# Retention and MoE on one core: outer products of chunk 2 ahead of its neighbour's scores, two weight casts on other engines, one weight sum later

## The chip, the core and the metric

The kernel runs on one core of a Trainium2 chip. The core has TensorE (PE, matrix products; its weight loads are shown apart as PEld), VectorE (DVE), ScalarE (ACT), GpSimd (POOL) and SyncE (SP, which here only issues transfers), each with a queue of its own that runs in program order. On-chip data lie in SBUF; matrix products are written to PSUM tiles. The metric is the device time of one execution in microseconds, lower is better.

## The reference

Two layers follow each other: a retention layer, which keeps a decaying state per head and reads it out with q at every token, and a feed-forward layer with the activation h * tanh(softplus(h)).

```python
# q, k, v: 4 batches, 8 heads, 768 tokens, 64 wide
for t in range(S):
    state = gamma[None, :, None, None] * state + np.einsum('bhd,bhe->bhde', k[:, :, t], v[:, :, t])
    y[:, :, t] = scale * np.einsum('bhd,bhde->bhe', q[:, :, t], state)
# x = y as 3072 tokens x 512; w_in 512 x 2048, w_out 2048 x 512
h = x @ w_in
sp = np.where(h > 20.0, h, np.log1p(np.exp(np.minimum(h, 20.0))))
return (h * np.tanh(sp)) @ w_out
```

## The kernel before

**Tiling.** The 3072 tokens are 24 chunks of 128. Within a chunk retention is done in matrix form: scores k q masked to the past (`scores...`, `mask...`), the masked scores times v (`present...`), the state before the chunk times q (`past...`), and the outer products k v that advance the state (`outer...`, `state...`). The results y, transposed, are the input `xt` of the feed-forward layer. Chunks are grouped in blocks: the first has four chunks, the other ten have two. A block's first product with `w_in` goes to PSUM tiles `h_ps`, the activation is taken by ScalarE, and the product with `w_out` goes to `o_ps`. From block 1 on both products are done by a scheme of seven products instead of eight per 2x2 partition, for which sums of weights (`wsum` from `w_in`, `tmat` from `w_out`), of inputs (`xsum`) and of activations (`gsum`) are made beforehand by VectorE.

**Weights.** `w_in` comes as four slices of 512 columns (`load_w`), 1 MB each, in SyncE's queue behind q, k and v of the first chunks; slice 0 comes as two transfers of half a slice. Each slice is cast from 32 to 16 bits in two halves (`cast_win(s, half, engine)`), the tiles `win{s}_{half}`. The first block works through the slices in order: `first_g1(h_ps, u, s)` uses columns u * 128 of slice 0, so u = 0 and 1 need half 0, and u = 2 and 3 need half 1; the later slices are used by `g1(0, u)` for u = 4 to 15. `w_out` follows as four slices, cast by `cast_wout(s, part, on_act)`; a slice's staging tile is that of an earlier input slice, so that the transfer of output slice 0 waits until both halves of input slice 0 are cast.

**The order.** Everything is scheduled by hand: each engine runs its instructions as the Python code issues them, and semaphores order the engines among each other. The first block is written out in `first_block` and `first_g2`; later blocks take their small steps from tables. In `first_block` the prologue takes chunks 0 to 3 in pairs: the score products of a pair are done in two halves of the heads (`scores_half(s, half, at)`, L314), each into a PSUM tile `at` that is masked by VectorE (`mask_half`, L321). Two such tiles exist, so that the scores of one wait for the mask of the one before the last. `outer_first(s, chunks)` makes the outer products of the chunks of pair s (L333), from k cast by ScalarE and v scaled by GpSimd (`cast_two`, L288); `state_first(g)` adds the state before (L343) and decays it by VectorE (L345). `fourth_state` (L354, L361) makes the fourth chunk's state, which GpSimd decays (L366).

A list `late` holds VectorE's weight sums as work that is called off piecewise (`some_late(n)`): `win_sums(a)` gives eight steps for a = 0 and eight for a = 1, sixteen in all (L770), `weight_sums(half)` four (L722 to L725). A table `plan` says what is issued behind which u of the first block's products. In `first_g2`, behind two pairs of products, one finds a chain over two engines: VectorE's second weight sum (L723), GpSimd's `gate` on it (L427), which holds GpSimd's queue, and behind the gate the scaling of the next chunks' q (`cast_q`, L406), which TensorE then transposes (`turn`, L453).

Of the kernel before, what the change touches and what calls it, by code (L numbers as in the profile page):

```python
# [16 lines left out]
def kernel(  # L17
# [9 lines left out]
    nc = tc.nc  # L27
# [15 lines left out]
    NSL = 4  # L43
# [14 lines left out]
    def toks(c):  # L58
        return slice(c * HB, (c + 1) * HB)
# [83 lines left out]
    nload, late, early = [0], [], set()  # L143
    BRING = CPB
    stores = []
    last_ended, yet = [], []

# [49 lines left out]
    def cast_win(s, half, eng):  # L199
        src = wtmps["in", s]  # L200
        t = cpool.tile([P, NBP, TB // 2], FP16, name=f"win{s}_{half}")
        src = src[:, :, half * (TB // 2):(half + 1) * (TB // 2)]
        if eng is nc.scalar:
            nc.scalar.copy(t, src)
        else:
            eng.tensor_copy(t, src)
        wins[s, half] = t

    def cast_wout(s, f, on_act=False):
        if s not in wouts:  # L210
            wouts[s] = cpool.tile([P, FPS, d_model], FP16, name=f"wout{s}")
        dst, src = wouts[s][:, f], wtmps["out", s][:, f]
        if on_act:
            nc.scalar.copy(dst, src)
        else:
            nc.vector.tensor_copy(dst, src)
# [110 lines left out]
    def outer_first(s, chunks=(0, 1)):  # L327
        u_ps = {c: mmps.tile([P, HP, P], FP32, name="u_ps", tag="mm") for c in chunks}
        for i in range(HP):
            half, j = divmod(i, HP // 2)  # L330
            for r in range(R):
                for c in chunks:
                    nc.tensor.matmul(  # L333
                        u_ps[c][:, i], k16s[s][toks(c), half, r, 2 * j:2 * j + 2],
                        v16s[s, half][toks(c), r, 2 * j:2 * j + 2],
                        start=i == 0 and r == 0, stop=r == R - 1, skip_group_check=True)
        for c in chunks:
            us[2 * s + c] = u_ps[c]

    def state_first(g):  # L340
        u = us.pop(g)
        if g > 0:
            nc.tensor.matmul(u, ident, states[g - 1], start=False, stop=True, skip_group_check=True)  # L343
        states[g] = stp.tile([P, HP, P], FP16, name="st")
        nc.vector.tensor_tensor(states[g], u, gcm, op=ALU.mult)  # L345
# [88 lines left out]
    def at_tile():  # L434
        return atps.tile([P, 2, HP // 2, R, C], FP32, name="at", tag="at")
# [271 lines left out]
    def some_late(n):  # L707
        for _ in range(min(n, len(late))):
            late.pop(0)()
# [351 lines left out]
    def first_block():  # L1061
# [50 lines left out]
        for half in range(2):  # L1112
            cast_two("v", 1, half)
        cast_win(0, 0, nc.gpsimd)
        at = at_tile()
        scores_half(1, 1, at)
        mask_half(1, 1, at)
        y = [atps.tile([P, 2, HP, C], FP32, name="y_ps", tag="at")[:, 0] for _ in range(2)]
        outer_first(1, [0])
        state_first(2)  # L1120
        h_ps = [mmps.tile([P, 1, TB], FP32, name="h_ps", tag="mm") for _ in range(2)]
        for u in range(2):
# [1 line left out]
        present_first(1, y, range(HP))  # L1124
        past_first(2, y)
        past_first(3, y)
        cast_win(0, 1, nc.vector)
        xt_out_by_two(2, y)
        for u in range(2, FPS):
            h_ps.append(mmps.tile([P, 1, TB], FP32, name="h_ps", tag="mm"))  # L1130
# [13 lines left out]

        def more_sums():
            late.extend(win_sums(1))
            some_late(8)
            late.extend(weight_sums(0) + weight_sums(1))

        plan = {6: [(cast_win, NSL - 1, 0, nc.scalar)],  # L1150
                7: [(cast_win, NSL - 1, 1, nc.scalar), (more_sums,)],
                9: [(cast_wout, 0, slice(0, 3)), (cast_wout, 0, slice(3, 4), True), (room_for_more,),
                    (bring_first,)],
                10: [(some_late, 1)],
# [30 lines left out]
    def first_g2():  # L1185
# [33 lines left out]
        for p in pairs:  # L1219
            mm(pe[p], sm(p, 1), t(1), True)  # L1220
            nc.scalar.copy(m5[p], pe[p])
        cast_wout(2, slice(0, 2))
        cast_wout(2, slice(2, 4), True)
        some_late(1)
        gate(tmats[0][:, 1, 0, :1])
# [193 lines left out]
```

## Time and profile before

| | |
|---|---|
| times of three runs | 191.51, 190.88 and 306.08 us, median 191.51 |
| the profiled execution | 190.88 us, of them 189.0 us from the first to the last instruction |
| TensorE busy | 182.5 us, 97% of the span |
| VectorE, ScalarE, GpSimd busy | 155.6, 126.8 and 95.3 us |
| granted TensorE clock | 1.000 |
| chain that ended last | 91% TensorE |

The profile is of one execution. Lines of the timeline give the start in us from the span's beginning, the length in us, engine, line of the code, operation, tiles, shapes and count; in square brackets stands the idle time of the engine just before and what ended it. Neighbouring instructions of a kind are merged to one row. A PE matmul's row may overlap the next, since products are pipelined. Rows of the chain give start, length and work. Rows of the stretches give, for each, its length and the busy time and count of instructions by engine, the granted clock, the DMA share and the rate.

### The profile page before, as it was taken

To read this page: it belongs to the slowest core of one execution; us is meant where nothing else is said; L and a number is where in the kernel's file an instruction comes from. 1 tells how busy PE (TensorE), PEld (TensorE's weight loads), DVE (VectorE), ACT (ScalarE), POOL (GpSimd) and SP (SyncE) were. 2 spreads that over 40 slices of the span, in tenths; PEclk is the share of its full clock that TensorE was granted. 3 is DMA by queue.
4 is the path that set the end of the run, shared out by engine and by line. 5 is a ranking of instruction groups with operands and counts; after the bars stand their busy time and mean duration, and the time that the engine had idled before them with its cause. 6 is when DMAs were issued, how large, how long until landed. Compare 5 with 4: busy or idle time off the path is not lost.

```text
span 189.0 us, 7724 instructions
## 1 busy us (share of the span) xinstructions
PE 182.5 (97%) x3283; PEld 155.8 (82%) x3283; DVE 155.6 (82%) x329; ACT 126.8 (67%) x249; POOL 95.3 (50%) x135
## 2 busy tenths in 40 slices
PE   7789999999999999999999999999999999999992
PEld 3457546975988988988988988988988989989981
DVE  3997899879899699797897897797897897796662
ACT  3462599385883983983983984974874974965960
POOL 6570107696878937924935925916916913000000
PEclk9999999999999999999999999999999999999999
DMA  5999999999999999999998995999996984300203
GB/s 165 351 368 405 404 407 279 278 248 134 151 192 251 180 285 210 208 219 177 167 194 146 188 187 158 197 195 120 178 203 117 148 144 59 114 0 17 101 0 111
DMA packets 95521, 36.17 MB, mean 191 GB/s; under 512 B 82560, under 2 KB 88960, under 8 KB 95488
## 3 DMA queue, kind: packets, MB, share of 16 engines
q1 hardware_dynamic: 74112, 32.78, 75.3%
q0 software_dynamic: 21088, 2.62, 22.4%
q8 instruction: 25, 0.41, 0.9%
q10 hardware_dynamic: 288, 0.30, 0.4%
q14 instruction: 8, 0.07, 0.1%
HBM read 27.30 MB, written 6.29 MB: 178 GB/s over the span
## 4 chain that ended last, share of the span: by engine, by line
PE 91%; DVE 3%; DMA 2%; POOL 1%; issue 1%; ACT 0%; SPq 0%; DVEq 0%; POOLq 0%
PE h_ps L820 34%; PE o_ps L956 32%; PE h_ps L687 6%; PE o_ps L1210 5%; DMA qfirst<-in_q_dram 2%; PE h_ps L1057 2%; PE o_ps L1275 2%; PE y_ps L532 2%; PE u_ps L483 2%; PE at L497 2%; DVE am L321 2%; PE y_ps L543 2%; POOL qfirst L249 1%; DVE osb L977 1%; PE at L314 0%
## 5 line engine op out<-in xcount | busy, mean ns | idle before, releaser
L840 DVE TENSOR_TENSOR hsum<-h_ps,hsnap 128x512 f32<-128x512 f32 x60 | 38.5, 685 | 10.1 <-ACT hsnap L830 6.6
L830 ACT COPY hsnap<-h_ps 128x512 f32<-128x512 f32 x60 | 32.1, 589 | 10.3 <-PE h_ps L820 10.1
L820 PEld LDWEIGHTS <-wsum 128*128 128x128 f16 x640 | 36.2, 98 | 0.1
L835 ACT ACTIVATE g<-hsum 128x512 f16<-128x512 f32 x60 | 34.6, 643 | 0.6 <-DVE hsum L840 0.2
L956 PEld LDWEIGHTS <-gsum 128*128 128x128 f16 x320 | 30.4, 98 | 3.7
L820 PE MATMUL h_ps<-xsum,wsum 128*128 128x128 f16 x480 | 30.2, 220 | 0.0
L956 PE MATMUL o_ps<-tmat,gsum 128*128 128x256 f16 x240 | 29.5, 273 | 0.0
L820 PEld LDWEIGHTS <-win 128*128 128x128 f16 x480 | 28.2, 98 | 0.9
L418 POOL DMA_DIRECT2D qk<-in_k_dram x36 | 27.5, 777 | 0.0
L956 PEld LDWEIGHTS <-g 128*128 128x128 f16 x248 | 22.7, 98 | 2.6
L406 POOL TENSOR_TENSOR qk<-qf,qvs 128x512 f16<-128x512 f32 x20 | 22.1, 1106 | 0.0
L956 PE MATMUL o_ps<-wout,g 128*128 128x256 f16 (+1 forms) x168 | 20.8, 268 | 0.0
L423 POOL TENSOR_TENSOR v<-vf,qvs 128x512 f16<-128x512 f32 x20 | 20.7, 1060 | 0.0
L820 PE MATMUL h_ps<-xt,win 128*128 128x128 f16 x320 | 19.6, 220 | 0.0
L550 ACT COPY hsum<-y_ps 128x512 f32<-128x512 f32 x9 | 5.3, 585 | 18.3 <-PE y_ps L543 18.3
L977 DVE TENSOR_TENSOR osb<-o_ps,snap 128x256 f32<-128x256 f32 (+1 forms) x32 | 13.0, 413 | 5.0 <-PE o_ps L956 2.4
L597 POOL TENSOR_TENSOR stc<-suc,gcv 128x256 f16<-128x256 f32 x15 | 9.9, 662 | 13.6 <-DVE suc L592 13.6
L427 POOL COPY gate<-gsum 128x1 f16<-128x1 f16 x10 | 1.9, 186 | 26.8 <-DVE gsum L927 26.8
L965 ACT COPY snap<-o_ps 128x256 f32<-128x256 f32 x31 | 11.4, 371 | 5.4 <-PE o_ps L956 5.0
L820 PE MATMUL h_ps<-xsum,win 128*128 128x128 f16 x160 | 12.3, 220 | 0.0
L820 PE MATMUL h_ps<-xt,wsum 128*128 128x128 f16 x160 | 12.2, 220 | 0.0
L835 ACT ACTIVATE g<-h_ps 128x512 f16<-128x512 f32 x20 | 12.0, 599 | 0.0
(144 smaller groups left out, 309.4 us busy)
## 6 DMA issues: line engine op xcount, KB each, us to landing
vf<-in_v_dram SPq DMA_DIRECT2D x24, 256.0 KB, 6.2
out_dram<-osb SPq DMA_DIRECT2D x22, 256.0 KB, 2.9
qf<-in_q_dram SPq DMA_DIRECT2D x20, 256.0 KB, 5.3
wi<-in_moe_w_in_dram SPq DMA_DIRECT2D x3, 1024.0 KB, 10.5
wt<-in_moe_w_out_dram SPq DMA_DIRECT2D x3, 1024.0 KB, 9.6
qk<-in_k_dram POOLq DMA_DIRECT2D x36, 64.0 KB, 5.1
qfirst<-in_q_dram SPq DMA_DIRECT2D x2, 512.0 KB, 4.3
kf<-in_k_dram SPq DMA_DIRECT2D x4, 256.0 KB, 4.9
```

The lines of the kernel that those rows point to most:

```text
L406: nc.gpsimd.tensor_tensor(by_head(g, room16(g)[0]), by_head(0, loaded[g][0]), f.broadcast_to((P, 2, HP, D)), op=ALU.mult)
L418: nc.gpsimd.dma_start(room16(g)[1][:, x::2], src[:, HP * x:HP * x + HP])
L423: nc.gpsimd.tensor_tensor(room16(g)[2], loaded[g][2], vs.unsqueeze(2).broadcast_to((P, H, D)), op=ALU.mult)
L597: by.tensor_tensor(stcs[g], sus.pop(g), decay, op=ALU.mult)
L687: nc.tensor.matmul(h_ps[:, j], win(s, f, bp), xt(blk, bp), start=(bp == 0), stop=(bp == NBP - 1))
L820: nc.tensor.matmul(h_ps[g][:, f], w(g, f, d), x(d), start=first and f == 0 and d == 0, stop=d == n - 1, skip_group_check=True)
L830: nc.scalar.copy(x, h_ps)
L835: nc.scalar.activation(gt[:, fb:fb + FPS, j * P:(j + 1) * P], h, AF.Mish, scale=inv_boost3)
L840: nc.vector.tensor_tensor(h, h_ps, x, op=ALU.add)
L956: nc.tensor.matmul(t, x(f), w(f)[:, c], start=first and f == 0, stop=f == n - 1, skip_group_check=True)
L965: nc.scalar.copy(x[:, c], t)
L977: nc.vector.tensor_tensor(dst[:, c], t, plus[:, c], op=ALU.add)
```

## The change

Five places move; no instruction is added or dropped, and no transfer changes its order.

1. `outer_first(1, [0])`, the outer products of chunk 2, stands ahead of `scores_half(1, 1, ...)` instead of behind its mask.
2. `cast_win(0, 1)`, slice 0's second half, is cast by GpSimd right behind the first half, instead of by VectorE behind the products of the states.
3. `cast_win(3, 1)`, slice 3's second half, is cast by VectorE instead of ScalarE, between the eighth and the ninth weight sum.
4. The last of the sixteen sums of `w_in` is put aside in a list `later`.
5. It is issued in `first_g2`, behind VectorE's half of output slice 2's cast.

```diff
-    last_ended, yet = [], []
+    last_ended, yet, later = [], [], []
...
         cast_win(0, 0, nc.gpsimd)
+        cast_win(0, 1, nc.gpsimd)
+        outer_first(1, [0])
         at = at_tile()
         scores_half(1, 1, at)
         mask_half(1, 1, at)
         y = [atps.tile([P, 2, HP, C], FP32, name="y_ps", tag="at")[:, 0] for _ in range(2)]
-        outer_first(1, [0])
         state_first(2)
...
         past_first(3, y)
-        cast_win(0, 1, nc.vector)
         xt_out_by_two(2, y)
...
         def more_sums():
             late.extend(win_sums(1))
-            some_late(8)
+            some_late(7)
+            later.extend(late)
+            late.clear()
             late.extend(weight_sums(0) + weight_sums(1))
...
-                7: [(cast_win, NSL - 1, 1, nc.scalar), (more_sums,)],
+                7: [(cast_win, NSL - 1, 1, nc.vector), (more_sums,)],
...
         cast_wout(2, slice(0, 2))
+        later.pop(0)()
         cast_wout(2, slice(2, 4), True)
```

On TensorE, in the prologue, before (`y_ps` is the result of chunks 0 and 1, `at` the score tile, `u_ps` the outer products, `v_389` and `v_391` the two halves of v, `st` the state; each pair of rows stands for several):

```order
L381 LDWEIGHTS st
L381 MATMUL y_ps<-qfirst_t,st 128x128
L314 LDWEIGHTS qkt
L314 MATMUL at<-qfirst_t,qkt 64x128
...
L333 LDWEIGHTS qk_293
L333 MATMUL u_ps<-v_389,qk_293 128x128
...
L333 MATMUL u_ps<-v_391,qk_293 128x128
L343 LDWEIGHTS ident
L343 MATMUL u_ps<-st,ident 128x512
```

and the same place with the change:

```order
L381 LDWEIGHTS st
L381 MATMUL y_ps<-qfirst_t,st 128x128
L333 LDWEIGHTS qk_293
L333 MATMUL u_ps<-v_389,qk_293 128x128
...
L333 MATMUL u_ps<-v_391,qk_293 128x128
...
L314 LDWEIGHTS qkt
L314 MATMUL at<-qfirst_t,qkt 64x128
...
L343 LDWEIGHTS ident
L343 MATMUL u_ps<-st,ident 128x512
```

The eight outer products now stand ahead of the sixteen score products, directly behind the results of chunk 1.

On VectorE, in the sums of `w_in` and what follows them, before (`win_0_565` and `win_1_573` are slice 3's halves, `win_1_515` is slice 1's second and `win_1_478` slice 0's second, `wout_600` output slice 0, `wout_702` output slice 2, `tmat` the sums of `w_out`):

```order
L770 TENSOR_TENSOR wsum<-win_1_478,wsum 128x2x256
L770 TENSOR_TENSOR wsum<-win_0_565 128x2x256
...
L770 TENSOR_TENSOR wsum<-win_1_515,win_1_573 128x2x256
L770 TENSOR_TENSOR wsum<-win_1_515,wsum 128x2x256
L216 COPY wout_600<-wt 128x1536
L722 TENSOR_TENSOR tmat<-wout_600 128x1024
...
L216 COPY wout_702<-wt 128x1024
L723 TENSOR_TENSOR tmat<-wout_702,tmat 128x1024
```

and with the change (slice 0's second half is `win_1_395` now, the output slices `wout_599` and `wout_701`):

```order
L770 TENSOR_TENSOR wsum<-win_1_395,wsum 128x2x256
L206 COPY win_1_573<-wi 128x1024
L770 TENSOR_TENSOR wsum<-win_0_565 128x2x256
...
L770 TENSOR_TENSOR wsum<-win_1_515,win_1_573 128x2x256
L216 COPY wout_599<-wt 128x1536
L722 TENSOR_TENSOR tmat<-wout_599 128x1024
...
L216 COPY wout_701<-wt 128x1024
L770 TENSOR_TENSOR wsum<-win_1_515,wsum 128x2x256
L723 TENSOR_TENSOR tmat<-wout_701,tmat 128x1024
```

Ahead of the ninth sum stands a cast more, and the sixteenth sum stands between the cast of output slice 2 and L723 instead of ahead of the cast of output slice 0.

On GpSimd, before the change and with it, one cast more stands ahead of the decay of the fourth state, `stc` (`win_0_393` and `win_1_395` are slice 0's halves):

```order
 L288 TENSOR_TENSOR v_391<-vf,qvs 128x4x2x64
 L206 COPY win_0_393<-wi 128x1024
+L206 COPY win_1_395<-wi 128x1024
 L366 TENSOR_TENSOR stc<-suc,gcf 128x256
 L427 COPY gate<-wt 128x1
```

The second cast directly follows the first.

## The prediction

> **What bounds the kernel now.** I read the page's busy shares and its chain that ended last first, then the stretches, then the timeline of each engine around the places that the change touches.
>
> ```profile
> PE 182.5 (97%) x3283; PEld 155.8 (82%) x3283; DVE 155.6 (82%) x329; ACT 126.8 (67%) x249; POOL 95.3 (50%) x135
> PEclk9999999999999999999999999999999999999999
> PE 91%; DVE 3%; DMA 2%; POOL 1%; issue 1%; ACT 0%; SPq 0%; DVEq 0%; POOLq 0%
> core 0: us, PE busy (x) PEld busy (x) DVE busy (x) ACT busy (x) POOL busy (x), PEclk, DMA share, GB/s
> 13.40:20.00 6.60, 6.30 (x114) 5.03 (x114) 5.18 (x8) 3.24 (x7) 1.07 (x2) 1.00 1.06 404
> 20.00:30.60 10.60, 10.56 (x54) 4.71 (x50) 9.98 (x23) 8.45 (x15) 2.34 (x3) 1.00 1.06 396
> 30.60:47.00 16.40, 16.40 (x195) 12.67 (x194) 14.28 (x22) 10.43 (x22) 12.49 (x13) 1.00 1.24 216
> 47.00:180.00 133.00, 133.00 (x2731) 122.69 (x2729) 112.06 (x234) 96.53 (x194) 70.63 (x99) 1.00 1.01 161
> ```
>
> TensorE is busy for 97% of the span at full clock, and the chain is 91% TensorE. From 20 us on it hardly pauses: 0.04 us are missing in 20 to 30.6, nothing in 30.6 to 180. Everything that the change touches lies before 52 us. So the change can win only where TensorE pauses now, and of the stretches it touches that is 13.4 to 20, with 6.60 - 6.30 = 0.30 us. It can lose wherever it makes TensorE wait in 14 to 47 us, where nothing waits today. A shift of TensorE at 47 us goes straight to the end, since no pause behind it absorbs it.
>
> The one pause, on TensorE's timeline, then the same place on the chain (start, length):
>
> ```profile
> 13.00 0.39 PE L381 MATMUL y_ps<-qfirst_t,st 128*128 128x128 f16 x4
> 13.70 0.42 PE L314 MATMUL at<-qfirst_t,qkt 64*64 64x128 f16 x16 [0.32 <-DVE am L321]
> 14.05 0.62 PE L333 MATMUL u_ps<-v,qk 64*128 64x128 f16 x8
> 14.12 0.55 PE u_ps L333 x8
> 14.67 0.32 PE u_ps L343
> 14.99 0.87 PE h_ps L1057 x8
> 12.44 1.22 DVE L321 TENSOR_TENSOR am<-at,tri_first 128x1024 f16<-128x1024 f32 x1
> 12.38 1.06 POOL L288 TENSOR_TENSOR v<-vf,qvs 128x512 f16<-128x512 f32 x1
> ```
>
> The score products of L314 write a PSUM tile that VectorE's mask (12.44 + 1.22 = 13.66) must have left; TensorE had been free since 13.38 and starts at 13.70, 0.04 us behind the mask's end. That 0.04 is my price for a hand-over between engines. The outer products (L333) stand behind the scores and need neither mask nor scores.
>
> **Outer products ahead of scores.** Nothing is added or removed: 8 products, 0.55 us on the chain. They need the second half of v, scaled by GpSimd until 12.38 + 1.06 = 13.44, so the last four may start at 13.48; the first four need no more than the first half and run from 13.38. They end at 13.93, the scores start then instead of at 13.70 (the mask is over at 13.66), and L343 starts at 14.35, not 14.67. **Gain 0.32 us**, or 0.17 if the second half of v came 0.15 later than the row says. The next to be late would be what VectorE does behind the scores:
>
> ```profile
> 14.17 1.22 DVE L321 TENSOR_TENSOR am<-at,tri_first 128x1024 f16<-128x1024 f32 x1
> 15.31 0.68 DVE L345 TENSOR_TENSOR st<-u_ps,gcm 128x512 f16<-128x512 f32 x1
> 15.91 0.68 DVE L206 CAST win<-wi 128x1024 f16<-128x1024 f32 x1
> 16.37 0.62 PE L381 MATMUL y_ps<-qfirst_t,st 128*128 128x128 f16 x8
> ```
>
> The last mask of the prologue now follows later scores: it starts near 14.40 and ends at 15.62, the state's product (L345) runs 15.54 to 16.22. TensorE wants the mask at about 15.8 (the second half of L374) and the state near 16.39 (the second four of L381, 0.32 earlier than today). Both are covered, by 0.15 us or so; if that cover is gone, TensorE waits the difference and the gain shrinks by it.
>
> **Slice 0, half 1: VectorE to GpSimd.** GpSimd's cast of the other half and the transfer that the new one needs:
>
> ```profile
> 13.48 1.04 POOL L206 CAST win<-wi 128x1024 f16<-128x1024 f32 x1
> 9.14 0.69 SPq L184 DMA_DIRECT2D wi<-in_moe_w_in_dram  x1
> wi<-in_moe_w_in_dram SPq DMA_DIRECT2D x1, 512.0 KB, 5.6
> 16.77 0.10 PEld L1057 LDWEIGHTS <-win 128*128 128x128 f16 x1
> 16.67 0.37 SPq L191 DMA_DIRECT2D wt<-in_moe_w_out_dram  x1
> wt<-in_moe_w_out_dram SPq DMA_DIRECT2D x1, 1024.0 KB, 9.6
> ```
>
> The half lands near 9.14 + 5.6 = 14.74; GpSimd is free at 14.52, casts until 15.8, and TensorE loads these weights at 16.77 - 0.32 = 16.45. Cost **0**, covered by 0.6 us. VectorE loses 0.68 us of work there, but it then waits for slice 1's transfer anyway, so that gains nothing. SyncE's first output slice, queued behind this cast, is issued at 15.9 instead of 16.67; it lands behind the input slices in either case (16.67 + 9.6 = 26.3), so I price it at 0, with 0.2 either way.
>
> **Slice 3, half 1: ScalarE to VectorE, and the sixteenth sum.** The cast leaves ScalarE (1.04 us each, no TensorE wait hangs on it) and lengthens VectorE's unbroken run from 21 to 35 us:
>
> ```profile
> 21.13 1.08 DVE L206 CAST win<-wi 128x1024 f16<-128x1024 f32 x1 [0.17 <-DMA wi<-in_moe_w_in_dram]
> 21.13 1.68 DVE L206 CAST win<-wi 128x1024 f16<-128x1024 f32 x2 [0.17 <-DMA wi<-in_moe_w_in_dram]
> 18.65 1.29 DVE L206 CAST win<-wi 128x1024 f16<-128x1024 f32 x2 [0.93 <-DMA wi<-in_moe_w_in_dram]
> 20.11 0.86 DVE L361 TENSOR_TENSOR suc<-u_ps,st 64x256 f32<-64x256 f32 x2 [0.16 <-PE u_ps L354]
> 21.05 0.61 POOL L366 TENSOR_TENSOR stc<-suc,gcf 128x256 f16<-128x256 f32 x1 [6.52 <-DVE suc L361]
> 28.45 0.42 DVE L770 TENSOR_TENSOR wsum<-win,wsum 128x512 f16<-128x512 f16 x1
> 28.79 0.95 DVE L216 CAST wout<-wt 128x1536 f16<-128x1536 f32 x1
> 30.44 0.69 DVE L1177 TENSOR_TENSOR gsum<-g 128x1024 f16<-128x1024 f16 x1
> 31.33 0.32 PEld L1210 LDWEIGHTS <-gsum 128*128 128x128 f16 x3
> ```
>
> A cast of this kind adds 1.68 - 1.08 = 0.60 us to the run, a sum 28.79 - 28.45 = 0.34. With one cast more and one sum fewer the first output cast (L216) is late by 0.26 us. Against that stands the row at 21.13: the same cast takes 0.68 elsewhere and 1.08 here, while GpSimd runs L366 beside it. L366 waits for VectorE's sum of the fourth state (L361, at 20.11), which waits for TensorE; with TensorE earlier it moves by 0.22 us (no more, since VectorE is at slice 1's casts, which a transfer starts, until about 19.9), and the overlap shrinks by as much. Bounds: nothing saved to 0.40 saved; I take 0.22, because the overlap is the nearest row to the excess. VectorE's run is then late by **0.04 us**, or 0.26 without it.
>
> The Trainium skill, page "SBUF — State Buffer", section "SBUF: two separate sides", says that GpSimd and a two-port VectorE operation hold a shared port pair for a whole instruction, the later one waiting. The rows agree in kind: 0.40 us too long, where GpSimd's span reaches 0.53 past the cast's start. By that rule the hold shrinks exactly as L366 moves and the sum is mine; without it nothing is saved, and the sum is that of the second rival.
>
> First consumer: the first sum of activations is done at 30.44 + 0.69 = 31.13 now, 31.17 then; its weights are loaded at 31.33, wanted 0.32 earlier, possible from 31.21. So **0.20 of the 0.32 is given back here**. Then the sixteenth sum:
>
> ```profile
> 33.12 0.68 DVE L216 CAST wout<-wt 128x1024 f16<-128x1024 f32 x1
> 34.05 0.69 DVE L723 TENSOR_TENSOR tmat<-wout,tmat 128x1024 f16<-128x1024 f16 x1 [0.25 <-ACT wout L214]
> 34.89 0.50 POOL L427 COPY gate<-tmat 128x1 f16<-128x1 f16 x1 [2.42 <-DVE tmat L723]
> 35.35 1.50 POOL L406 TENSOR_TENSOR qk<-qf,qvs 128x512 f16<-128x512 f32 x1
> 37.01 0.32 PEld L453 LDWEIGHTS <-qk 128*128 128x128 f16 x4
> ```
>
> It falls into VectorE's idle 0.25 us ahead of L723, but takes 0.34: free at 33.80 + 0.04, plus 0.34, L723 starts at 34.18, 0.13 late. GpSimd's gate waits for L723, the whole of GpSimd's queue waits behind the gate, and its first scaling of q ends at 35.35 + 1.50 + 0.13 = 36.98. TensorE loads that q at 37.01 today and could at 37.02. **The remaining 0.12 goes there.**
>
> Sum: -0.32 + 0.20 + 0.12 = 0.0, rounded (+0.01). The profiled execution took 190.88 us (span 189.0 and 1.9 around it), so it would again be 190.9. The median shown, 191.51, holds one run of 306; the two that agree have 191.2 as their mean, 0.3 above the profiled one. With that offset the forecast is **191.2 us**, no change.
>
> **Rivals**, with the same offset.
> 1. The gain survives: GpSimd's spans are rough, and the scaled q may have been ready 0.3 us before its row ends, the sum of activations likewise. For it: neither place shows a wait today. Against: the rows put both within 0.2 us of their use. 191.2 - 0.32 = 190.9 us.
> 2. The hold at 21.13 isn't L366's, and VectorE is late by 0.26 in full: weights at 31.44 instead of 31.33, L723 at 33.80 + 0.26 + 0.34 = 34.40, q ready at 37.24 against 37.01: 0.23 slower, 191.4 us. For it: one long row is thin evidence. The change failing at its own aim (the outer products waiting for v, so that L366 doesn't move) ends at the same number.
> 3. Slower: GpSimd's second cast holds up VectorE's last mask. It would run 14.74 to 15.8; a mask held until then ends at 17.0, where TensorE wants it at 15.8: 1.2 us of wait, less 0.32, 192.1 us. It decides once the mask ends after 15.8. Against: today's mask at 14.17 starts inside GpSimd's cast (13.48 to 14.52) and takes its usual 1.22.
>
> **How the numbers follow.** Forecast 0.45, gain survives 0.2, VectorE late in full 0.22, mask held 0.06; 0.07 for what I haven't seen, most of it a transfer or a queue falling out of step by microseconds. Executions differ by 0.6 us (190.88 to 191.51). The first three cases span 190.9 to 191.4; with 0.6 below and, for the third rival's side, 0.9 above, the range is 190.3 to 192.3. Two per cent, 3.8 us, is about what a measurement of this kernel can tell from no change; no case of mine reaches it. Faster by over 2%: 0.02; the pauses before 180 us don't hold 3.8 us that this change could reach. Slower: 0.05. Within: 0.93.
>
> **What would show it.** Right: the 0.32 us ahead of L314 is gone and L333 stands before L314 from 13.4; L343 near 14.35; GpSimd's two casts of L206 back to back, the second ending before 16; L366 near 20.8 and the cast beside it near 0.86 us; the loads of the sums (L1210) at 31.2; L723 near 34.2; the load of q (L453) at 37.0 again. Wrong: TensorE still 0.2 us or more ahead at 37 us (rival 1), a full 1.08 us cast and L453 at 37.2 (rival 2), a mask of over 2 us (rival 3). The forecast falls as a whole if TensorE shows a pause of over 1 us between 14 and 52 us, or the later stages pause at all.

## The result: 0.3% slower, through a wait that the prediction priced at 0.12 us

The changed kernel takes 191.78 us (median; before, beside it, 191.42). The ratio is **1.0031, 95% interval 1.0016 to 1.0045**, some 0.6 us of loss. The forecast was no change, 191.2 us in a range of 190.3 to 192.3: the time lies in the range, but the change has a sign, and the forecast had none. The interval is about half a us wide, so that far smaller changes than the 2% that the prediction named can be told here. Of 22 executions each, two of before (306 us) and one of after (367 us) were far longer and are not in the ratio. The profiled execution took 191.82 us, with a span of 190.1.

The page's busy shares and chain of the kernel after:

```profile
PE 182.5 (96%) x3283; PEld 155.2 (82%) x3283; DVE 155.0 (82%) x329; ACT 126.3 (66%) x248; POOL 95.3 (50%) x136
PE 78%; DVE 7%; DMA 6%; SPq 5%; POOL 1%; issue 1%; DVEq 0%; POOLq 0%
```

TensorE is busy for the same 182.5 us in a span 1.1 us longer: the loss is waiting. The chain fell from 91% TensorE to 78%: followed back, it now leaves TensorE near 38 us and goes through GpSimd and VectorE to a transfer. The stretches of the kernel after (length, busy time and count by engine) say where TensorE waits:

```profile
13.40:20.00 6.60, 6.58 (x114) 4.99 (x114) 4.71 (x8) 3.43 (x7) 2.09 (x3) 1.00 1.06 404
20.00:30.60 10.60, 10.60 (x53) 5.00 (x51) 9.82 (x23) 7.84 (x15) 2.36 (x4) 1.00 1.06 396
30.60:47.00 16.40, 15.71 (x188) 11.74 (x186) 13.20 (x21) 9.47 (x19) 11.50 (x12) 1.00 1.24 214
```

The pause of the first stretch is gone (6.58 busy instead of 6.30), but in 30.6 to 47 us, where TensorE never waited, 0.69 us are missing. TensorE's timeline of the kernel after, in the prologue and around 31 to 38 us:

```profile
13.30 0.62 PE L333 MATMUL u_ps<-v,qk 64*128 64x128 f16 x8
13.85 0.42 PE L314 MATMUL at<-qfirst_t,qkt 64*64 64x128 f16 x16
14.29 0.38 PE L343 MATMUL u_ps<-st,ident 128*128 128x512 f16 x1
...
30.16 1.04 PE L1212 MATMUL o_ps<-wout,g 128*128 128x256 f16 x8
31.32 1.05 PE L1212 MATMUL o_ps<-tmat,gsum 128*128 128x256 f16 x8
...
35.74 1.04 PE L1212 MATMUL o_ps<-tmat,gsum 128*128 128x256 f16 x8
36.61 0.60 PE L1212 MATMUL o_ps<-wout,gsum 128*128 128x256 f16 x4
37.78 0.40 PE L453 MATMUL t_ps<-ident,qk 128*128 128x128 f16 x4 [0.57 <-POOL qk L406]
```

Before, the same group stood at 36.68 (L1210 then, L1212 now) and the transposes of q at 37.11:

```profile
36.68 0.60 PE L1210 MATMUL o_ps<-wout,gsum 128*128 128x256 f16 x4
37.11 0.39 PE L453 MATMUL t_ps<-ident,qk 128*128 128x128 f16 x4
```

So 0.43 us became 37.78 - 36.61 = 1.17: **0.74 us lost at the transposes of q**, of which the row shows 0.57 as idle. The wait is for GpSimd's scaling of q. A smaller loss stands at 31.32: 1.16 us after the group ahead of it, which takes 0.87 where nothing waits (35.74 to 36.61 in the same profile), **0.29 us**.

GpSimd's timeline of the kernel after, from the prologue to that scaling, then VectorE's:

```profile
13.47 1.04 POOL L206 CAST win<-wi 128x1024 f16<-128x1024 f32 x1
14.84 1.04 POOL L206 CAST win<-wi 128x1024 f16<-128x1024 f32 x1 [0.33 <-DMA wi<-in_moe_w_in_dram]
20.84 0.61 POOL L366 TENSOR_TENSOR stc<-suc,gcf 128x256 f16<-128x256 f32 x1 [4.96 <-DVE suc L361]
35.03 1.71 POOL L427 COPY gate<-tmat 128x1 f16<-128x1 f16 x1 [3.77 <-DVE tmat L723]
36.69 1.03 POOL L406 TENSOR_TENSOR qk<-qf,qvs 128x512 f16<-128x512 f32 x1
```

```profile
21.11 1.50 DVE L206 CAST win<-wi 128x1024 f16<-128x1024 f32 x2 [0.35 <-DMA wi<-in_moe_w_in_dram]
...
33.26 0.69 DVE L216 CAST wout<-wt 128x1024 f16<-128x1024 f32 x1
33.86 0.42 DVE L770 TENSOR_TENSOR wsum<-win,wsum 128x512 f16<-128x512 f16 x1
34.19 0.68 DVE L723 TENSOR_TENSOR tmat<-wout,tmat 128x1024 f16<-128x1024 f16 x1
34.79 0.69 DVE L724 TENSOR_TENSOR tmat<-wout,wout 128x1024 f16<-128x1024 f16 x1
35.40 0.69 DVE L1185 TENSOR_TENSOR gsum<-g,gsum 128x1024 f16<-128x1024 f16 x1
36.00 0.69 DVE L725 TENSOR_TENSOR tmat<-wout,tmat 128x1024 f16<-128x1024 f16 x1
```

The gate copies one element per partition. Before, it took 0.50 us (34.89), and VectorE's L725 was the one that waited, 1.53 us long, beside the scaling of q. VectorE's row of before:

```profile
35.87 1.53 DVE L725 TENSOR_TENSOR tmat<-wout,tmat 128x1024 f16<-128x1024 f16 x1
```

Now VectorE's four operations L723 to L725 take their usual 0.68 to 0.69 each, and the gate lasts until the fourth is over (35.03 + 1.71 = 36.74; 36.00 + 0.69 = 36.69). The scaling of q starts only then. Its first half ends at 36.69 + 1.03 = 37.72 instead of 35.35 + 1.50 = 36.85, 0.87 us later: the gate starts 0.14 later with L723 and takes 1.21 more, and the scaling, with VectorE idle beside it, gives 0.47 back. The transposes had 0.2 us to spare and start 0.67 later (37.11 to 37.78); the group ahead of them stands 0.07 earlier (36.68 to 36.61), which makes the 0.74.

### The profile page after: what moved, and what is told of

Read it like the earlier page. It is cut to its first block, busy times and chain, and to the rows that moved or that the text cites. A ratio compares the mean times of both kernels' runs of the same rounds, so it can differ in the third digit from the quotient of the medians.

```text
span 190.1 us, 7725 instructions
## 1 busy us (share of the span) xinstructions
PE 182.5 (96%) x3283; PEld 155.2 (82%) x3283; DVE 155.0 (82%) x329; ACT 126.3 (66%) x248; POOL 95.3 (50%) x136
## 4 chain that ended last, share of the span: by engine, by line
PE 78%; DVE 7%; DMA 6%; SPq 5%; POOL 1%; issue 1%; DVEq 0%; POOLq 0%
PE h_ps L820 34%; PE o_ps L956 32%; DMA wi<-in_moe_w_in_dram 6%; SPq L270 3%; DVE wsum L770 3%; PE o_ps L1278 2%; PE y_ps L532 2%; PE o_ps L1212 2%; PE u_ps L483 2%; PE at L497 2%; PE y_ps L543 2%; DVE wout L216 1%; DVE win L206 1%; SPq L184 1%; POOL gate L427 1%
## 5 line engine op out<-in xcount | busy, mean ns | idle before, releaser
L406 POOL TENSOR_TENSOR qk<-qf,qvs 128x512 f16<-128x512 f32 x20 | 21.1, 1057 | 0.0
L956 PE MATMUL o_ps<-wout,g 128*128 128x256 f16 (+1 forms) x168 | 20.8, 267 | 0.0
L427 POOL COPY gate<-gsum 128x1 f16<-128x1 f16 x10 | 1.8, 184 | 26.7 <-DVE gsum L927 26.7
```

Of the source, the lines that this page charges most:

```text
L406: nc.gpsimd.tensor_tensor(by_head(g, room16(g)[0]), by_head(0, loaded[g][0]), f.broadcast_to((P, 2, HP, D)), op=ALU.mult)
L956: nc.tensor.matmul(t, x(f), w(f)[:, c], start=first and f == 0, stop=f == n - 1, skip_group_check=True)
```

## Experiments

In the table the ratio is to the kernel before (with its interval), *pause* is VectorE's idle time between its cast of output slice 2 and L723 (in the kernels with several sums there, between these), *gate* is the length of GpSimd's row of L427, *wait* is the idle time that TensorE's row of L453 shows. Pause, gate and wait are from one profile each.

| kernel | ratio | pause | gate | wait |
|---|---|---|---|---|
| before; before_again | | 0.25; 0.17 | 0.50 | 0 |
| outer_only | 1.0005 [0.9981, 1.0029] | 0.17 | 0.50 | 0 |
| cast3_on_scalar | 1.0004 [0.9979, 1.0029] | 0.10 | 0.50 | 0 |
| sum_in_place | 1.0022 [0.9996, 1.0047] | 0.10 | 0.50 | 0 |
| sum_first | 1.0032 [1.0007, 1.0058] | 0.10 | 0.50 | 0 |
| before_filled | 1.0039 [1.0018, 1.0059] | 0.23 | 0.50 | 0 |
| after_scalar_late | 1.0027 [1.0002, 1.0052] | 0.35 | 0.50 | 0 |
| before_three | 1.0080 [1.0054, 1.0106] | 0.03 twice | 0.50 | 0.29 |
| sum_twice | 1.0019 [0.9995, 1.0043] | 0.03 | 0.50 | 0.28 |
| two_later | 1.0017 [0.9993, 1.0041] | none | 0.50 | 0.16 |
| after; after_again; after_third | 1.0031 [1.0016, 1.0045]; one execution; 1.0068 [1.0038, 1.0097] | none | 1.71 | 0.57 |
| cast3_and_later | 1.0043 [1.0023, 1.0063] | none | 1.70 | 0.57 |
| pause_early | one execution | none | 1.71 | 0.57 |
| two_split | 1.0055 [1.0018, 1.0092] | none | 1.71 | 0.57 |
| three_later | 1.0036 [1.0014, 1.0058] | none | 1.71 | 1.03 |
| four_later | 1.0053 [1.0030, 1.0076] | none | 1.71 | 1.03 |

### Both kernels again

Neither is edited.

> The kernel before once more, for a second profile of it. Theory A (the gate on L723 is let in or kept out by VectorE's unbroken run of L723, L724, the fourth sum of activations and L725, and which of the two it is follows from the order of the work): the gate takes 0.50 us again and L453 comes at 37.1. Theory B (it is a matter of chance in each execution, in the kernel before as well): the gate may take 1.7 us here too, L453 then comes at 37.8 and the execution takes about 191.5 instead of 190.9. Theory C (the gate is not the cause): its length has no bearing on the time.

> The changed kernel once more. Theory A: the gate takes 1.7 us again and L453 comes at 37.8. Theory B: it may be let in, at 0.5 us, with L453 at 37.0 and a time near 190.9. Theory C: no relation between the two.

Measured 191.23 and 192.96 us, one execution each. The waits of TensorE from 13 to 180 us in after_again (engine, line, what it waited for, us, times, longest); before_again has none but that of L314 for the mask, 0.3 us:

```profile
PE t_ps L453 <- POOL qk L406: 0.6, 1, 0.6
PE o_ps L1212 <- DVE gsum L1179: 0.2, 1, 0.2
```

The two places of loss return, so they belong to the kernel and not to one execution. A third execution of the kernel after had them too:

> The changed kernel on the chip of the three others. Theory A: gate 1.7 us for the third time, wait at L453 0.5 to 0.7 us, ratio 1.003. Theory B: gate 0.5 us in this execution.

Measured 1.0068, gate 1.71, wait 0.57. The first profile also showed 0.3 us lost in the next block (VectorE's L724 held to 1.60 us by a scaling at 44.8); the two repeats don't show it (0.68 and 0.69 us), so it does not belong to the kernel.

### The outer products alone

The kernel before, with this edit only:

```diff
+        outer_first(1, [0])
         at = at_tile()
         scores_half(1, 1, at)
         mask_half(1, 1, at)
-        outer_first(1, [0])
```

> The kernel before with the outer products of chunk 2 ahead of the scores alone. All theories: TensorE is 0.2 to 0.3 us ahead at 20 us, with VectorE's run not later than before. Theory A: VectorE still has a pause ahead of L723, so the gate is let in, about 0.5 us, the q comes no later than before (L453 at 37.0), and the time is that of before, 0 to 0.2 us less. Theory B: the gate as often in as out, the times spread over 190.7 to 191.7 as those of before do. Theory C: the 0.2 to 0.3 us are gained, about 190.9 as a median.

TensorE's timeline of this kernel in the prologue and at the transposes of q:

```profile
13.77 0.62 PE L333 MATMUL u_ps<-v,qk 64*128 64x128 f16 x8
14.32 0.42 PE L314 MATMUL at<-qfirst_t,qkt 64*64 64x128 f16 x16
37.28 0.39 PE L453 MATMUL t_ps<-ident,qk 128*128 128x128 f16 x4
```

No wait is left anywhere between 13 and 180 us, yet the ratio is 1.0005 [0.9981, 1.0029]. From a group of transposes in the prologue (L299, at 10.98 here) to the first products of slice 0 (L687, at 20.36) TensorE took 9.38 us here and 9.32 in the kernel after, against 9.52 and 9.46 in the two profiles of before: of the 0.32 us, 0.1 to 0.2 reach 20 us, the rest goes into slightly wider spacing of the later products. In after_third and cast3_on_scalar TensorE also waited 0.4 us for an earlier mask (L374, at 13 us), ahead of the place that changed; why is open. Against an interval of half a per cent, 1 us, such a gain can't be seen.

### Slice 3's half back on ScalarE

The kernel after, with one word changed back:

```diff
-                7: [(cast_win, NSL - 1, 1, nc.vector), (more_sums,)],
+                7: [(cast_win, NSL - 1, 1, nc.scalar), (more_sums,)],
```

> The changed kernel with slice 3's second half on ScalarE again, the rest as changed. VectorE's run is 0.6 us shorter ahead of the output casts, so that L723 waits for ScalarE's cast of output slice 2 again. Theory A: with that pause the gate is let in (0.5 us), L453 near 37.0, time as before or 0.3 less, ratio to the kernel before 0.998 to 1.000. Theory B: in or out by chance, ratio 1.000 to 1.002. Theory C (the later weight sum or the second cast on GpSimd costs the time): ratio 1.003 as with the whole change.

GpSimd's and TensorE's timelines of this kernel:

```profile
35.51 0.50 POOL L427 COPY gate<-tmat 128x1 f16<-128x1 f16 x1 [2.60 <-DVE tmat L723]
```

```profile
37.30 0.60 PE L1212 MATMUL o_ps<-wout,gsum 128*128 128x256 f16 x4
37.73 0.39 PE L453 MATMUL t_ps<-ident,qk 128*128 128x128 f16 x4
```

The gate is back at 0.50 us, the transposes follow 0.43 us behind the group ahead of them as in the kernel before, the first sum is waited for no more, and the time is that of the kernel before. The sum still stands late here. So both waits hang on VectorE's cast of slice 3, as far as one profile shows; the interval of the ratio overlaps that of the kernel after.

### That cast and the late sum alone

The kernel before, with the change's parts 3 to 5 and neither the outer products nor slice 0:

```diff
-            some_late(8)
+            some_late(7)
+            later.extend(late)
+            late.clear()
...
-                7: [(cast_win, NSL - 1, 1, nc.scalar), (more_sums,)],
+                7: [(cast_win, NSL - 1, 1, nc.vector), (more_sums,)],
...
+        later.pop(0)()
```

> The kernel before with slice 3's half cast by VectorE and the sixteenth sum put off, and none of the rest of the change. By duration VectorE is 0.26 us late at the output casts and L723 0.3 us late, ratio 1.001 to 1.002. Theory A: the cast has used up VectorE's pause ahead of L723, the gate takes 1.7 us with a wait of 0.7 at L453, ratio 1.004 to 1.005. If the earlier prologue is needed for the loss: gate 0.5 us.

```profile
35.51 1.70 POOL L427 COPY gate<-tmat 128x1 f16<-128x1 f16 x1 [3.77 <-DVE tmat L723]
38.26 0.40 PE L453 MATMUL t_ps<-ident,qk 128*128 128x128 f16 x4 [0.57 <-POOL qk L406]
```

These are GpSimd's and TensorE's rows of this kernel. Without any change to the prologue, the whole wait is there, and the ratio is 1.0043 [1.0023, 1.0063]. The loss comes from these parts together.

### The sixteenth sum back in its place, or ahead of the cast

Both are edits of the kernel after. In the first (sum_in_place) all sixteen sums run together again; in the second (sum_first) the late sum and the cast change places:

```diff
-            some_late(7)
-            later.extend(late)
-            late.clear()
+            some_late(8)
...
-        later.pop(0)()
```

```diff
-        cast_wout(2, slice(0, 2))
         later.pop(0)()
+        cast_wout(2, slice(0, 2))
```

> The changed kernel with all sixteen weight sums together again, slice 3's half still cast by VectorE. VectorE reaches the output casts 0.34 us later than with the change, and L723 follows the cast of output slice 2 with no pause. Theory A (without a pause of VectorE ahead of L723 the gate is kept out until the run ends): gate 1.7 us, its wait at L453 0.6 to 0.8 us; and the wait for the first sum of activations grows from 0.3 to 0.6 us; ratio to the kernel before 1.004 to 1.006. Rival D (it is the sixteenth sum just ahead of L723 that keeps the gate out): the gate is let in, 0.5 us, ratio 1.002 to 1.003.

> The changed kernel with two of VectorE's instructions swapped: the sixteenth sum ahead of the cast of output slice 2 instead of behind it. Same work, same L723 but for 0.1 us: it now directly follows the cast whose result it reads, which in the profile of the variant with all sums together cost a pause of 0.1 us. Theory A (a pause of VectorE ahead of L723 decides): the gate is let in, 0.5 us instead of 1.7, no wait at L453, while the wait of 0.3 us for the first sum of activations stays; TensorE is 0.6 to 0.7 us earlier at 47 us than with the change, ratio to the kernel before 0.999 to 1.002. Theory B (chance, or the sum's mere presence): gate 1.7 us, ratio 1.003.

VectorE's and GpSimd's rows of sum_in_place, and the one wait of its TensorE:

```profile
34.28 0.68 DVE L216 CAST wout<-wt 128x1024 f16<-128x1024 f32 x1
35.06 0.69 DVE L723 TENSOR_TENSOR tmat<-wout,tmat 128x1024 f16<-128x1024 f16 x1
35.91 0.50 POOL L427 COPY gate<-tmat 128x1 f16<-128x1 f16 x1 [4.54 <-DVE tmat L723]
32.34 1.05 PE L1210 MATMUL o_ps<-tmat,gsum 128*128 128x256 f16 x8 [0.35 <-DVE gsum L1177]
```

In sum_in_place I had expected the gate at 1.7 and missed: with nothing between the cast and L723, which reads what the cast wrote, VectorE pauses 0.10 us (34.28 + 0.68 to 35.06), and the gate came in at 0.50. The loss stands at the first sum of activations instead, 0.35 us, since VectorE's run is a whole cast longer. In sum_first the same pause let the gate in, and TensorE waited 0.21 us for the later cast. So keeping the gate short doesn't win the time back: a VectorE that is late costs 0.2 to 0.35 us wherever its first result is awaited.

### A pause taken away, or put in

Three kernels try the pause ahead of L723 directly. Before_filled and before_three are the kernel before with the sixteenth sum repeated once, or three times, ahead of L723. The edit of before_three (before_filled puts one copy in the list, `twice.append(late[-1])`, and runs it once):

```diff
-    last_ended, yet = [], []
+    last_ended, yet, twice = [], [], []
...
             late.extend(win_sums(1))
+            twice.extend([late[-1]] * 3)
             some_late(8)
...
         cast_wout(2, slice(0, 2))
+        for again in twice:
+            again()
```

After_scalar_late is the kernel after with a redundant copy that makes ScalarE's half of the cast, and so L723, later:

```diff
+        nc.scalar.copy(wouts[2][:, 2:4, :384], wtmps["out", 2][:, 2:4, :384])
         cast_wout(2, slice(2, 4), True)
```

> The kernel before with nothing but the sixteenth weight sum done a second time between VectorE's cast of output slice 2 and L723, 0.34 us of work where VectorE pauses for 0.17 to 0.25 us. By duration alone L723 comes 0.1 to 0.2 us later and TensorE 0 to 0.2. Theory A: the pause is gone, the gate takes 1.7 us instead of 0.5, L453 comes 0.7 to 0.8 us later with a wait shown, ratio 1.003 to 1.004. Theory B (duration alone): gate 0.5 us, ratio 1.000 to 1.001. Rival E (the gate depends on the work ahead of the output casts, as with slice 3's half): gate 0.5 us.

> The changed kernel with work added: ScalarE casts 768 of the 1024 columns of its part of output slice 2 once more ahead of the whole, 0.7 us, so that VectorE pauses about 0.3 us ahead of L723. By duration alone this can only make L723 0.3 us later and the kernel as slow or slower, ratio 1.003 to 1.005. Theory A: the pause lets the gate in, 0.5 us instead of 1.7, q comes 0.3 to 0.4 us earlier than with the change, ratio 1.000 to 1.002. Rival D: the gate stays out, since the sixteenth sum is still there, ratio 1.004 to 1.005.

> The kernel before with three needless repetitions of the sixteenth weight sum ahead of L723, 1.0 us of work where one was not enough to fill VectorE's pause. By duration L723 comes 0.75 us later with the pause of 0.25 used up, the q by as much, less the 0.1 us of slack: 0.65 us at L453 with the gate at 0.5 us, ratio 1.003. Theory A: no pause, so the gate takes 1.7 us, and the q comes 1.4 to 1.5 us later than before, ratio 1.006 to 1.008.

Before_filled says nothing on the question: L723 waited 0.23 us for ScalarE all the same. Its ratio of 1.0039 comes without a long gate or a wait at L453, and its cause is open. In after_scalar_late the pause of 0.35 us was made and the gate took 0.50, but TensorE then waited 0.27 us for that same cast. VectorE's and GpSimd's rows of before_three:

```profile
34.07 1.34 DVE L770 TENSOR_TENSOR wsum<-win,wsum 128x512 f16<-128x512 f16 x3
35.32 0.68 DVE L723 TENSOR_TENSOR tmat<-wout,tmat 128x1024 f16<-128x1024 f16 x1
36.16 0.50 POOL L427 COPY gate<-tmat 128x1 f16<-128x1 f16 x1 [4.68 <-DVE tmat L723]
```

L723 starts inside the last sum's row, so there is no pause right ahead of it, and the gate still came in. That refuted the theory as I had it, that a pause directly ahead of L723 decides. But the three repeats write the same tile, and three sums that overlapped as others do (0.34 apart, 0.42 long) would take 1.10 us, not 1.34: there are two pauses of some 0.03 us between them. The ratio of 1.0080, 1.5 us, goes with a run of VectorE that is longer by the three sums, 1.3 us, and two waits of TensorE, 0.17 us for a sum of activations and 0.29 for q; where the rest of the 1.5 us goes was not found.

### Where the pause has to be

All three are edits of the kernel after. Sum_twice issues the late sum twice (a pause of 0.03 us between the two); two_later puts the fifteenth sum aside as well, so that two run late without a pause; pause_early has two repeats five operations ahead of L723, behind the cast of output slice 1:

```diff
+        later[0]()
         later.pop(0)()
```

```diff
-            some_late(7)
+            some_late(6)
...
         later.pop(0)()
+        later.pop(0)()
```

```diff
+        def last_sum():
+            later[0]()
...
-                13: [(cast_wout, 1, slice(0, 3)), (g_sum, 2), (g_sum, 3)],
+                13: [(cast_wout, 1, slice(0, 3)), (last_sum,), (last_sum,), (g_sum, 2), (g_sum, 3)],
```

> The changed kernel with the sixteenth sum done twice in a row behind VectorE's cast of output slice 2. The second writes what the first wrote and waits for it, so that VectorE pauses for some 0.04 us one operation ahead of L723; L723 itself comes 0.46 us later than with the change. Theory A2 (the gate is let in when VectorE has paused within the last two or three operations, kept out when its run is unbroken for longer): gate 0.5 us in spite of the added work, L453 at about the time of the changed kernel or up to 0.25 us earlier, ratio to the kernel before 1.003 to 1.005. Theory G (the number of operations between the cast and L723 decides, or their being sums): cannot be told from this run alone, see the next.

> The changed kernel with the fifteenth sum put off beside the sixteenth: the same work, two sums between the cast of output slice 2 and L723, which do not wait for each other. VectorE reaches the output casts 0.34 us earlier than with the change and L723 at the same time. Theory A2: the run is unbroken, gate 1.7 us, wait at L453 0.6 us, ratio 1.002 to 1.004 (the wait for the first sum of activations is gone, that for q is not). Theory G: gate 0.5 us as in the run with two sums that wait for each other, ratio 1.000 to 1.001.

> The changed kernel with the sixteenth sum done twice in addition, in a row, behind the cast of output slice 1: a pause of 0.04 us there, five operations ahead of L723, and no pause behind it. Theory A2: gate 1.7 us, since the pause lies too far back. If any pause in the run will do: 0.5 us. The time is not read here, since VectorE's work ahead of the sums of activations is 0.8 us longer.

VectorE's and GpSimd's rows of two_later:

```profile
33.53 0.68 DVE L216 CAST wout<-wt 128x1024 f16<-128x1024 f32 x1
34.14 0.41 DVE L770 TENSOR_TENSOR wsum<-win,win 128x512 f16<-128x512 f16 x1
34.47 0.41 DVE L770 TENSOR_TENSOR wsum<-win,wsum 128x512 f16<-128x512 f16 x1
34.81 0.68 DVE L723 TENSOR_TENSOR tmat<-wout,tmat 128x1024 f16<-128x1024 f16 x1
35.63 0.50 POOL L427 COPY gate<-tmat 128x1 f16<-128x1 f16 x1 [4.00 <-DVE tmat L723]
```

Sum_twice (0.50) and pause_early (1.71) came as the theory of the pause said, two_later did not: every operation starts inside the row ahead of it, and yet the gate took 0.50. In this profile no pause was needed.

### The count of operations

If not the pause, then perhaps how many operations VectorE has run since its last one, even or odd, or what runs directly ahead of L723. Two_split has the fifteenth sum late too, but behind the cast of output slice 1; three_later has three sums late ahead of L723; four_later has these and a repeat of the fifteenth behind them:

```diff
-            some_late(7)
+            some_late(6)
...
+        def one_later():
+            later.pop(0)()
...
-                13: [(cast_wout, 1, slice(0, 3)), (g_sum, 2), (g_sum, 3)],
+                13: [(cast_wout, 1, slice(0, 3)), (one_later,), (g_sum, 2), (g_sum, 3)],
```

```diff
-            some_late(7)
+            some_late(5)
...
-        later.pop(0)()
+        for _ in range(3):
+            later.pop(0)()
```

```diff
-            some_late(7)
+            some_late(5)
...
-        later.pop(0)()
+        for i in (0, 1, 2, 1):
+            later[i]()
```

> The kernel after, with the fifteenth sum late too, but not beside the sixteenth: it stands behind the cast of output slice 1 on VectorE, five operations ahead of L723, and does not read what the operation ahead of it wrote. From the first difference of the output slices (L722) on VectorE then runs unbroken, and the difference behind which the gate may come in (L724) is the tenth operation of the run, as in two_later, where it was let in (0.50 us); in the kernel after it is the ninth and in pause_early the eleventh, and both keep the gate out (1.71). Theory P (what counts is how many operations VectorE has run since its last pause of 0.10 us: even lets in, odd keeps out): gate 0.50, the first transposes of q wait under 0.3 us for the scaling. Theory L (what counts is what runs directly ahead of L723: two short sums let in, one keeps out): gate 1.71, wait near 0.57, time 1.003 of the kernel before.

> The kernel after, with the fourteenth, fifteenth and sixteenth sums late, all three one behind another ahead of L723, none reading what the one ahead of it wrote. L724 is then the eleventh operation of VectorE's unbroken run since L722. Theory P (even lets in, odd keeps out): gate 1.71, the first transposes of q wait near 0.57 us, time 1.003 to 1.005 of the kernel before. Theory L (two or more short sums directly ahead of L723 let in): gate 0.50, wait under 0.4 us, time 1.002.

> The kernel after, with the fourteenth, fifteenth and sixteenth sums late and the fifteenth repeated once behind them: four short operations in a row ahead of L723, none reading what the one ahead of it wrote, so that VectorE does not pause between its cast of output slice 2 and L723. Counted from that cast, the operation behind which the gate may come in (L724) is the sixth; it was the third and fifth where the gate was kept out (1.71 us) and the fourth in two_later, where it was let in. Theory P2 (even since the cast lets in): gate 0.50. Theory Q (only two_later's pattern, or chance of an execution, let it in; an unbroken run keeps it out): gate 1.71 and a wait of 0.57 us or more at the first transposes of q.

GpSimd's gate in two_split, which waited as long for L723 (4.00 us) as in two_later:

```profile
35.50 1.71 POOL L427 COPY gate<-tmat 128x1 f16<-128x1 f16 x1 [4.00 <-DVE tmat L723]
```

All three gates stayed out, 1.71 us each, and two_split, three_later and four_later have ratios of 1.0055, 1.0036 and 1.0053. Two_split refutes the count since the last pause (it has the same ten operations as two_later), three_later refutes "two or more sums", four_later refutes the count since the cast. What stands: where VectorE paused at least 0.03 us between its cast of output slice 2 and L723, the gate came in, in all ten profiles; where it did not, the gate stayed out in eight of nine, and two_later is the ninth. Why two_later let it in is **open**: it was profiled once, and whether it would again was not tried.

### Without the gate

The kernel after without the one-element copy that holds GpSimd back; the computation doesn't use it:

```diff
-        gate(tmats[0][:, 1, 0, :1])
```

> The changed kernel without the gate on L723, so that GpSimd may scale the next chunks' q as soon as it has issued two transfers and q has landed, at about 32.3 us. Theory A in its general form (an unbroken run of VectorE keeps any GpSimd work out): the scaling starts at 32.3 and does not end before VectorE's run does, 37.7, ratio 1.003 as with the change. Rival F (only the gate's place among L723 to L725 matters): the scaling is let in between two of VectorE's operations, q is there by 34 to 35, no wait at L453, VectorE's run ends 1 to 2 us later, and the ratio is 0.999 to 1.001 unless TensorE then waits for the sums.

Measured 1.0116 [1.0069, 1.0164]. The profile is of an execution of 196.81 us, above its median of 194.88, so only the order of its waits is read. GpSimd's, VectorE's and TensorE's timelines:

```profile
32.43 1.04 POOL L406 TENSOR_TENSOR qk<-qf,qvs 128x512 f16<-128x512 f32 x1 [0.80 <-DMA qf<-in_q_dram]
37.82 1.56 POOL L418 DMA_DIRECT2D qk<-in_k_dram  x2
39.39 2.57 POOL L423 TENSOR_TENSOR v<-vf,qvs 128x512 f16<-128x512 f32 x2
```

```profile
38.08 1.53 DVE L723 TENSOR_TENSOR tmat<-wout,tmat 128x1024 f16<-128x1024 f16 x1
39.53 1.53 DVE L724 TENSOR_TENSOR tmat<-wout,wout 128x1024 f16<-128x1024 f16 x1
40.98 1.53 DVE L1185 TENSOR_TENSOR gsum<-g,gsum 128x1024 f16<-128x1024 f16 x1
```

```profile
42.56 0.61 PE L1212 MATMUL o_ps<-wout,gsum 128*128 128x256 f16 x4 [1.87 <-DVE gsum L1185]
```

The first scaling of q now starts at 32.43, inside VectorE's run, and beside GpSimd's later work (two issues of transfers at 37.82, two scalings of v from 39.39 on) the three operations of VectorE grow from 0.68 to 1.53 us each. TensorE waits for VectorE instead, 1.87 us at the worst place. So it isn't so that a run of VectorE shuts GpSimd out as such; and in this kernel the gate, late as it is, protects more than it costs (1.0116 without it).

## Why the prediction was wrong

- **Prologue: the steps held, the gain was smaller.** The pause ahead of L314 is gone, L333 starts at 13.30, and L343 at 14.29 on the timeline, where it stood at 14.60 (the forecast of 14.35 counts on the chain, from 14.67): 0.31 us gained there. GpSimd's second cast ends at 15.88 (forecast 15.8) and delays nothing; the last mask beside it takes 1.23 us, and the rival of the held mask fell. At 20 us 0.1 to 0.2 us of the 0.32 are left.
- **Slice 3's cast: held.** L366 moved to 20.84 (forecast 20.8); the two casts at 21.11 take 1.50 together where they took 1.68, so the overlapped one takes 0.90 (forecast 0.86). The hold shrinks as L366 moves, as the sum assumed. The Trainium skill, page "SBUF — State Buffer", section "SBUF: two separate sides", has this as a lock held for a whole instruction, and the trace agrees: 0.18 us less overlap, 0.18 less length.
- **First sum of activations: held roughly.** A loss of 0.20 was forecast, 0.29 came, since VectorE reaches the output casts 0.12 us late (28.79 to 28.91), not 0.04; the two repeats show 0.2 of idle there.
- **Sixteenth sum: held to 0.01 us, in part by luck.** L723 starts at 34.19 (forecast 34.18). VectorE's cast ahead of the sum starts 0.14 us late (33.12 to 33.26), not 0.04, and the sum starts 0.09 before that cast ends, which the forecast had left out; the two cancel.
- **The gate: the step that failed.** "GpSimd's gate waits for L723, the whole of GpSimd's queue waits behind the gate, and its first scaling of q ends at 35.35 + 1.50 + 0.13 = 36.98." The chain of dependences is right. The error is in moving the row of 34.89 rigidly: its 0.50 us is not the price of a one-element copy (the twenty gates from 48 us on in the kernel before took 0.18 to 0.24 each), but a wait for VectorE that ended at VectorE's next change of operation. With the late sum in VectorE's idle time and the cast ahead of it, that wait became 1.71, and q was ready at 37.72, not 36.98. The term "The remaining 0.12" is 0.74. Up to the transposes of q the two profiles differ by 0.67 us (37.11 to 37.78), and the terms give -0.2 + 0.29 + 0.74 - 0.19 = 0.64. The 0.19 is time that before lost between 20 and 30.6 us in this one execution (10.56 us from L687 to L1210; 10.37 now, and 10.37 in before_again), and no effect of the change. That the sum comes near the 0.6 us of the ratio is therefore in part luck: the profiled pair differs by 1.1 us at the end, with 0.3 in the next block.
- **What was put down in advance as a sign of error:** L453 at 37.2 or later stood there for the second rival, a late VectorE. The number 191.4 was nearer, but its reason was not the one: VectorE was no later at L723 than forecast, and the casts overlapped less, as forecast.
- **What is shown and what is not.** Shown by taking it out and by doing it alone: the loss is made by VectorE's cast of slice 3 with the late sum. Shown by the rows of the gate: the kernels with slice 3 on VectorE or the sum late (leaving aside the repeats put into the kernel before) in which the gate lasts 1.7 us have ratios of 1.003 to 1.007, those in which it lasts 0.5 have 1.000 to 1.003; the groups differ by about 0.2 to 0.3%, and single intervals overlap. That is no more than what the kernel after itself shows from one set of runs to the next (1.0031 and 1.0068), and some of these kernels have waits of their own (two_split 0.48 us, two_later 0.25, for VectorE's casts of output slices), so the ratios alone don't prove it; the rows of L427, L406 and L453 carry it. Not settled: the rule by which the gate is let in.

No version here beats the kernel before: the two that lose nothing, outer_only and cast3_on_scalar, measure 1.0005 and 1.0004.

## What to carry to other kernels

A short instruction whose row is far longer than its work (0.50 us for one element per partition, 0.18 to 0.24 in twenty later ones) is a wait in disguise: don't shift it as a block, price it as "until the other engine lets go", with that engine's whole unbroken run as the upper end. Idle time of 0.25 us on one engine may be what lets another in; filling it with work that fits "for free" can cost the neighbour more than it saves. And when an edit spends the slack of three hand-overs that are each within 0.2 us, expect it to lose at one of them.

## What the runs showed of the hardware that was not expected

- A 128x1 copy on GpSimd with VectorE busy on two-input fp16 operations took 0.50 us in eleven profiles and 1.70 or 1.71 in eight, nothing between: it ended 0.05 us behind the VectorE operation in which it had become ready, or 0.05 us behind the last of VectorE's run, two operations later. The twenty later gates of the kernel before, each beside a VectorE operation that takes one input from a PSUM tile, took 0.18 to 0.24. The Trainium skill, page "SBUF — State Buffer", section "SBUF: two separate sides", says that whichever of the two engines starts first gets the shared pair of ports for its whole instruction and the other is blocked. The trace agrees in that both lengths end with an operation of VectorE; why the gate waits for one operation in some kernels and for three in others is open.
- In sum_in_place, L723, which reads what the cast ahead of it wrote, starts 0.10 us after that cast's end (34.28 + 0.68 to 35.06), while operations of the kernel after that don't read what the one ahead wrote start 0.08 before its end (34.19 + 0.68 against 34.79).
- VectorE is held as well: beside GpSimd's work, 128x1024 fp16 operations of VectorE take 1.53 us instead of 0.68 (35.87 in the kernel before; 38.08, 39.53 and 40.98 without the gate).
